# Loads at the start of a transformer block: three through GpSimd's DMA queue, and larger single DMAs for x and the key weights

## The chip, the cores and the metric

The kernel runs on one core of a Trainium2 chip. The metric is device time in microseconds, from the start of the program to its end. A core has five engines that run side by side, each with its own instructions in a fixed order: TensorE (matrix products; PE in the profile, its weight loads PEld), VectorE (DVE), ScalarE (ACT), GpSimd (POOL) and SyncE (SP), which here only starts DMA transfers. Engines wait for each other through semaphores. A transfer is started by one of the engines (its queue) and then moved by 16 DMA engines that all queues share.

## The reference

One transformer block with adaptive layer norm. x has 2048 tokens of 512 values, all in bf16.

```python
mod = (silu(c) @ w_mod).reshape(1, 6, 1, -1)          # c: 1 x 512, w_mod: 512 x 3072
sa, ca, ga, sb, cb, gb = mod[:, 0], ..., mod[:, 5]
h = layernorm(x) * (1 + ca) + sa
x = x + ga * attention(h, wqkv, w_phi, wo)
h = layernorm(x) * (1 + cb) + sb
x = x + gb * ((silu(h @ w_gate) * (h @ w_up)) @ w_down)
```

The attention is linear: 32 heads of 16 values. Queries and keys go through w_phi (16 x 16 for each head), then through two softmaxes over these 16 values, one of them with the sign turned; keys times values are summed over all tokens, and each query reads that sum.

## The kernel before

**Tiles and stages.** The tokens are cut into four chunks of 512 (`x_ch[0]` to `x_ch[3]`), each of four tiles of 128. In the first stage w_phi is folded into the key and the query weights (`fold_phi`: transposes at line 540, products at line 551), x is normalized (`first_norm`), transposed by TensorE (`first_T`, line 447) and scaled and shifted by `modA`, which holds 1 + ca and sa as columns. Then each tile gives its keys (line 613), values (line 617) and its share of the sum of keys times values (line 649), and each chunk its queries (line 673). The second stage is attention, output projection, second norm and the feed-forward network, which takes most of the time (lines 906 and 978).

**What stands first on TensorE.** Products of c with a one turn the row c into columns (line 471, `f_cT`); then w_phi is spread over the partitions (line 519, `f_phx`), the key weights are transposed in four groups (line 540), and the first fold is made (line 551). Then follow the four steps that make `modA` out of w_mod's first part, one for each block of 128 rows of w_mod (line 492, `mod_cols`), mixed with two more folds; then the first transposes of normalized x (line 447). Without modA no `hT`, the transposed and scaled x, can be written, and without `hT` no projection can start.

**The planner.** Each engine's order is not found on the chip: `Plan.run` walks a list, `ORDER`, and gives every operation a planned start, from the planned ends of what it needs, from the durations written at each operation (`us=`), and from the due times (`at`) of what is loaded. A due time comes from `load`: it adds up the bytes of the loads in the order in which they stand in the program, at 315 GB/s until 8 us and at 375 GB/s after that, from 3.1 us on, whichever queue the load goes to. c and w_phi have fixed due times, 4.5 and 4.1. The order of an engine's work does not depend on due times, since `ORDER` sets it.

**The filler.** Before each step of TensorE, `fill` puts matmuls of a tile of ones (line 1046) whose result is not used; they keep TensorE busy while it would wait. How many there are is fixed when the program is built, from the gap between the planned end of the step before and the planned start of this one:

```python
left = int((o.start - t0 + 0.05) * (1200 if t0 < 7.0 else 2400))
while left >= 64:
    fns.append(lambda n=min(left, CW): f(n))
    left -= CW
```

`left` counts columns, `CW` is 512, `t0` is the planned end of the step before. This form is used until the first product of keys and values (line 649).

**Loads.** ScalarE's queue starts w_phi and c. SyncE's queue starts, in this order: the first chunk of x in two halves, the key weights in two halves, w_mod's first part (columns 0 to 1023, the shift and the scale of the first norm) in four blocks of rows, the value weights, the second chunk of x in two halves, the query weights, the third and the fourth chunk of x. The wait of a step is on all that it reads: the transposes of key weights at line 540 need the half that holds their rows, the statistics of x at line 384 need the half of the chunk that holds their tile, and the steps at line 492 need silu(c) and their block of w_mod. The transposes of the query weights are DMA transposes on SyncE's queue (line 321), behind these loads.

Of the kernel before, what the change touches and what calls it, by code (L numbers as in the profile page):

```python
# [20 lines left out]
D = 512  # L21
KD = D // P
# [183 lines left out]
def kernel(  # L206
# [14 lines left out]
    nc = tc.nc  # L221
    ctx.enter_context(tc.manual_schedule())

    x_v = A_x.flatten_outer_dims().rearrange("(c p t) d -> c p t d", p=P, t=TPC)
    out_v = out.flatten_outer_dims().rearrange("(c p t) d -> c p t d", p=P, t=TPC)
    wqkv_v = A_wqkv.rearrange("(k p) n -> p k n", p=P)
    wmod_v = w_mod.rearrange("(k p) n -> p k n", p=P)
# [46 lines left out]
    x_ch = [attn.tile([P, TPC, D], BF16, name=f"x_c{i}") for i in range(NCH)]  # L274
    wqkv_sb = wts.tile([P, KD, 3 * D], BF16, name="wqkv_sb")
# [6 lines left out]
    wphi_sb = wts.tile([P, KD * DH], BF16, name="wphi_sb")  # L282
    c_row = const.tile([1, D], BF16, name="c_row")
# [3 lines left out]
    wmod_sb = modp.tile([P, KD, 6 * D], BF16, name="wmod_sb")  # L287
# [5 lines left out]
    def load(eng, dst, src, kb):  # L293
        eng.dma_start(dst, src)
        landed[0] += kb * 1024 / (315e3 if landed[0] < 8 else 375e3)
        return landed[0]

    nc.scalar.dma_start(wphi_sb[:], A_w_phi.rearrange("h (q t) f -> (h q) (t f)", t=4))
    nc.scalar.dma_start(c_row[:], c[:, :])
    at_x = {}  # L300
    at_x[0, 0] = load(nc.sync, x_ch[0][:, 0:2, :], x_v[0][:, 0:2, :], 256)
    at_x[0, 1] = load(nc.sync, x_ch[0][:, 2:4, :], x_v[0][:, 2:4, :], 256)
    at_wk = [load(nc.sync, wqkv_sb[:, i:i + 2, D:2 * D], wqkv_v[:, i:i + 2, D:2 * D], 256) for i in range(0, KD, 2)]
    at_m1 = [load(nc.sync, wmod_sb[:, k, 0:2 * D], wmod_v[:, k, 0:2 * D], 256) for k in range(KD)]
    landed[0] += 0.9
    at_wv = load(nc.sync, wqkv_sb[:, :, 2 * D:3 * D], wqkv_v[:, :, 2 * D:3 * D], 512)
    at_x[1, 0] = load(nc.sync, x_ch[1][:, 0:2, :], x_v[1][:, 0:2, :], 256)
    at_x[1, 1] = load(nc.sync, x_ch[1][:, 2:4, :], x_v[1][:, 2:4, :], 256)
    at_wq = load(nc.sync, wqkv_sb[:, :, 0:D], wqkv_v[:, :, 0:D], 512)
    at_x[2] = load(nc.sync, x_ch[2][:], x_v[2], 512)  # L310
    at_x[3] = load(nc.sync, x_ch[3][:], x_v[3], 512)
# [29 lines left out]
    nc.gpsimd.memset(mhalf[:], -0.5)  # L341
    eps_t = const.tile([P, 1], FP32, name="eps")
    nc.gpsimd.memset(eps_t[:], LN_EPS)

    nc.scalar.add_instruction(mybir.InstLoadActFuncSet(name=nc.get_next_instruction_name(), act_func_set_id=6,
                                                       ins=[], outs=[]))
# [365 lines left out]
    for i in range(NT):  # L712
        c_i, t = divmod(i, TPC)
# [372 lines left out]
```

The softmax here doesn't subtract the row's maximum and nothing guards it: scores larger than these inputs give would overflow.

## Time and profile before

| | before |
|---|---|
| time, median of 2 runs | 208.63 us (208.31 to 208.96) |
| span of the profiled execution | 207.3 us |
| TensorE busy (fillers included) | 202.4 us, 98% |
| VectorE, ScalarE, GpSimd busy | 143.1, 114.0, 131.0 us |
| filler at line 1046 in the first 30 us | 13.3 us |
| key weights, first half, started and landed | 1.64 us, 6.19 us |
| first step of w_mod on TensorE (line 492) | 8.7 us |
| first projection (line 617) | 13.2 us |

A busy TensorE is not a useful TensorE here: the fillers count as busy. The chain of waits, which follows the work that ended last back to the start, says what each stretch of time hangs on. The timeline lists instructions in order of time, runs of equal ones merged: start, duration, engine, line, operation, tile written and tiles read, sizes, and how many.

### The profile page before, as it was taken

The numbers are of one execution on the slowest core, as the hardware profiler recorded it, in microseconds if no ns is written. First come the engines' busy times: TensorE is split into PE (matmuls) and PEld (weight loads), VectorE is DVE, ScalarE is ACT, GpSimd is POOL, SyncE is SP. The second block draws the span as 40 slices with busy tenths as digits, with TensorE's granted clock in tenths as the row PEclk, the third lists the DMA queues.
The fourth block names the chain that finished last, engine by engine and source line by source line (L and its number), as shares of the span: only waits on it lengthen the run. The fifth ranks groups of instructions, "written<-read, shape, count | busy, mean of one in ns | idle before, by whom it ended". The sixth has DMA issues, their size and how long they took to land.

```text
span 207.3 us, 4949 instructions
## 1 busy us (share of the span) xinstructions
PE 202.4 (98%) x1876; PEld 140.0 (68%) x1876; DVE 143.1 (69%) x351; ACT 114.0 (55%) x244; POOL 131.0 (63%) x172
## 2 busy tenths in 40 slices
PE   7999999999999999999999999999999999999994
PEld 2764656454555698785887876879675787698752
DVE  6699899999676886999789687887467222322232
ACT  2689999998789974335452542422532564044300
POOL 1069999899991546689678793677749254061451
PEclk9999999999999999999999999999999999999999
DMA  5996993797000011231611233202321330020012
GB/s 176 335 389 119 321 191 87 275 406 254 4 0 0 3 25 36 51 81 26 91 32 28 58 83 81 57 0 60 79 62 28 79 85 3 13 66 27 0 34 68
DMA packets 34025, 19.76 MB, mean 95 GB/s; under 512 B 25073, under 2 KB 30674, under 8 KB 34002
## 3 DMA queue, kind: packets, MB, share of 16 engines
q1 hardware_dynamic: 33712, 19.38, 33.5%
q8 instruction: 14, 0.23, 0.5%
q10 hardware_dynamic: 290, 0.08, 0.2%
q14 instruction: 9, 0.07, 0.1%
HBM read 11.58 MB, written 2.10 MB: 66 GB/s over the span
## 4 chain that ended last, share of the span: by engine, by line
PE 92%; DMA 2%; ACT 1%; POOL 1%; DVE 1%; SPq 0%; issue 0%; DVEq 0%
PE one_ps L906 34%; PE one_ps L978 18%; PE one_ps L852 7%; PE one_ps L613 6%; PE one_ps L673 6%; PE one_ps L617 5%; PE four_ps L781 4%; PE one_ps L948 3%; PE kv_ps L1046 2%; DMA wqkv_sb<-in_A_wqkv_dram 2%; PE kv_ps L649 2%; PE one_ps L447 1%; PE one_ps L551 1%; PE one_ps L540 1%; ACT e L624 1%; POOL phik L642 1%
## 5 line engine op out<-in xcount | busy, mean ns | idle before, releaser
L978 PE MATMUL one_ps<-wd_sb,gu 128*128 128x512 bf16 (+2 forms) x176 | 41.0, 372 | 0.0
L906 PE MATMUL one_ps<-hT,wg_sb 128*128 128x256 bf16 (+1 forms) x400 | 41.0, 251 | 0.0
L906 PE MATMUL one_ps<-hT,wu_sb 128*128 128x256 bf16 (+1 forms) x400 | 40.9, 251 | 0.0
L913 ACT ACTIVATE sg<-one_ps 128x512 bf16<-128x512 f32 (+1 forms) x42 | 23.7, 576 | 27.6 <-PE one_ps L906 26.4
L906 PEld LDWEIGHTS <-wg_sb 128*128 128x128 bf16 x400 | 32.7, 98 | 4.8
L906 PEld LDWEIGHTS <-wu_sb 128*128 128x128 bf16 x400 | 32.9, 98 | 4.2
L916 DVE TENSOR_TENSOR gu<-one_ps,sg 128x512 bf16<-128x512 f32 (+1 forms) x26 | 16.6, 640 | 22.1 <-PE one_ps L906 12.8
L642 POOL TENSOR_TENSOR phik<-e,R 128x1024 bf16<-128x1024 bf16 x16 | 30.5, 1930 | 1.1 <-ACT eT L679 0.7
L922 POOL TENSOR_TENSOR gu<-usb,sg 128x512 bf16<-128x512 bf16 x16 | 18.5, 1155 | 16.8 <-ACT sg L913 13.3
L978 PEld LDWEIGHTS <-gu 128*128 128x128 bf16 (+1 forms) x187 | 17.7, 98 | 15.0
L384 DVE BATCH_NORM_STATS2 st<-x_c 128x6 f32<-128x512 bf16 x32 | 21.3, 682 | 1.4 <-DMA x_c<-in_A_x_dram 1.1
L994 POOL TENSOR_TENSOR ot<-x_c,fg 128x512 bf16<-128x512 bf16 (+1 forms) x14 | 15.7, 1118 | 8.8 <-DVE fg L990 8.8
L839 POOL TENSOR_TENSOR o<-o 128x512 bf16<-128x512 bf16 x14 | 16.1, 1154 | 7.6 <-DVE o L819 7.1
L819 DVE TENSOR_TENSOR o<-four_ps,A 128x512 bf16<-128x512 f32 x32 | 20.5, 683 | 0.0
L634 DVE TENSOR_REDUCE S<-e 128x64 f32<-128x1024 bf16 x16 | 19.0, 1194 | 0.6 <-ACT e L624 0.4
L624 ACT ACTIVATE e<-one_ps 128x512 bf16<-128x512 f32 x32 | 17.7, 631 | 1.6 <-POOL phik L642 1.0
L990 DVE TENSOR_TENSOR fg<-one_ps,gab 128x512 bf16<-128x512 f32 (+1 forms) x16 | 10.7, 672 | 11.5 <-PE one_ps L978 10.8
L679 ACT ACTIVATE eT<-one_ps 128x512 bf16<-128x512 f32 x32 | 17.5, 628 | 1.4 <-PE one_ps L673 1.3
L920 ACT CAST usb<-one_ps 128x512 bf16<-128x512 f32 x16 | 9.3, 586 | 16.3 <-PE one_ps L906 14.4
L852 PE MATMUL one_ps<-wo_sb,oT 128*128 128x512 bf16 x64 | 16.1, 379 | 0.0
L617 PE MATMUL one_ps<-wqkv_sb,hT 128*128 128x512 bf16 x64 | 15.9, 379 | 0.1
L673 PE MATMUL one_ps<-hT,Wq 128*128 128x512 bf16 x64 | 15.6, 379 | 0.1
(117 smaller groups left out, 311.2 us busy)
## 6 DMA issues: line engine op xcount, KB each, us to landing
wmod_sb<-in_w_mod_dram SPq DMA_DIRECT2D x2, 1024.0 KB, 7.0
out_dram<-ot SPq DMA_DIRECT2D x15, 128.0 KB, 2.0
wg_sb<-in_B_w_gate_dram SPq DMA_DIRECT2D x1, 1376.0 KB, 8.3
wu_sb<-in_B_w_up_dram SPq DMA_DIRECT2D x1, 1376.0 KB, 11.3
wd_sb<-in_B_w_down_dram SPq DMA_DIRECT2D x1, 1280.0 KB, 14.4
x_c<-in_A_x_dram SPq DMA_DIRECT2D x4, 256.0 KB, 4.7
wmod_sb<-in_w_mod_dram SPq DMA_DIRECT2D x4, 256.0 KB, 5.7
wqkv_sb<-in_A_wqkv_dram SPq DMA_DIRECT2D x2, 512.0 KB, 7.1
```

The lines of the kernel that those rows point to most:

```text
L384: pl.op("DVE", r=reads, w=[st6], us=0.6, fn=lambda: nc.vector.bn_stats(st6()[:], src))
L617: nc.tensor.matmul(v()[:], lhsT=hT[c_i][k][:, cols], rhs=wqkv_sb[:, k, 2 * D:3 * D], start=(k == 0), stop=(k == KD - 1))
L624: nc.scalar.activation(e()[:, :, sg].rearrange("p g h f -> p g (h f)"), pk()[:].rearrange("p (g n) -> p g n", g=G), ACT.Exp, scale=(1.0, - ...
L634: pl.op("DVE", r=[e], w=[Ss], us=1.14, fn=lambda: nc.vector.tensor_reduce(Ss()[:], e()[:].rearrange("p g s h f -> p (g s h) f"), axis=AX.X ...
L642: pl.op("POOL", r=[e, R], w=[bphik[i]], us=1.92, fn=lambda: nc.gpsimd.tensor_tensor(bphik[i]()[:].rearrange("p g s h f -> p (g s h) f"), e ...
L673: nc.tensor.matmul(pq()[:], lhsT=Wq2[:, k, j * P:(j + 1) * P], rhs=hT[c_i][k][:], start=(k == 0), stop=(k == KD - 1))
L819: nc.vector.tensor_tensor(o2()[:, sg].rearrange("p j (h d) -> p j h d", d=DH), ndv()[:, :, sg, 0:P].rearrange("p j (h d) -> p j h d", d=DH ...
L852: nc.tensor.matmul(a()[:], lhsT=oT()[:, j, :], rhs=wo_sb[:, j, :], start=(j == 0), stop=(j == KD - 1))
L906: nc.tensor.matmul(ps_()[0:fsz, q * n:(q + 1) * n], lhsT=wt[:, k, m * P:m * P + fsz], rhs=h2[k], start=(k == 0), stop=(k == KD - 1))
L913: pl.op("ACT", r=[g, btab], w=[sg], us=0.08 + 0.41 * L / CW, fn=lambda: nc.scalar.activation(sg()[0:fsz, 0:L], g()[0:fsz, 0:L], ACT.Silu))
L922: pl.op("POOL", r=[usb, sg], w=[gu], us=0.17 + 0.98 * L / CW, fn=lambda: nc.gpsimd.tensor_tensor(gu()[0:fsz, 0:L], usb()[0:fsz, 0:L], sg() ...
L978: nc.tensor.matmul(fp()[:], lhsT=b()[0:fsz, c0:c0 + P], rhs=wd_[0:fsz, m, wcs], start=(m == 0), stop=(m == FM - 1))
```

## The change

Four loads leave their queues. c and w_phi go from ScalarE's queue to GpSimd's, behind GpSimd's few constants. w_mod's first part goes from SyncE's queue to GpSimd's, in two halves instead of four blocks; its lines also move to a later place in the program, behind all first loads of SyncE. The first chunk of x, the second chunk of x and the key weights are loaded in one DMA each instead of two. The purpose is to have fewer and larger transfers at the start, and to let a third queue start some of them, so that SyncE and ScalarE get to their next work sooner.

```diff
-    nc.scalar.dma_start(wphi_sb[:], A_w_phi.rearrange("h (q t) f -> (h q) (t f)", t=4))
-    nc.scalar.dma_start(c_row[:], c[:, :])
     at_x = {}
-    at_x[0, 0] = load(nc.sync, x_ch[0][:, 0:2, :], x_v[0][:, 0:2, :], 256)
-    at_x[0, 1] = load(nc.sync, x_ch[0][:, 2:4, :], x_v[0][:, 2:4, :], 256)
-    at_wk = [load(nc.sync, wqkv_sb[:, i:i + 2, D:2 * D], wqkv_v[:, i:i + 2, D:2 * D], 256) for i in range(0, KD, 2)]
-    at_m1 = [load(nc.sync, wmod_sb[:, k, 0:2 * D], wmod_v[:, k, 0:2 * D], 256) for k in range(KD)]
+    at_x[0, 0] = at_x[0, 1] = load(nc.sync, x_ch[0][:], x_v[0], 512)
+    at_wk = [load(nc.sync, wqkv_sb[:, :, D:2 * D], wqkv_v[:, :, D:2 * D], 512)] * 2
     landed[0] += 0.9
     at_wv = load(nc.sync, wqkv_sb[:, :, 2 * D:3 * D], wqkv_v[:, :, 2 * D:3 * D], 512)
-    at_x[1, 0] = load(nc.sync, x_ch[1][:, 0:2, :], x_v[1][:, 0:2, :], 256)
-    at_x[1, 1] = load(nc.sync, x_ch[1][:, 2:4, :], x_v[1][:, 2:4, :], 256)
+    at_x[1, 0] = at_x[1, 1] = load(nc.sync, x_ch[1][:], x_v[1], 512)
     at_wq = load(nc.sync, wqkv_sb[:, :, 0:D], wqkv_v[:, :, 0:D], 512)
     at_x[2] = load(nc.sync, x_ch[2][:], x_v[2], 512)
     at_x[3] = load(nc.sync, x_ch[3][:], x_v[3], 512)
...
     eps_t = const.tile([P, 1], FP32, name="eps")
     nc.gpsimd.memset(eps_t[:], LN_EPS)
+    nc.gpsimd.dma_start(c_row[:], c[:, :])
+    nc.gpsimd.dma_start(wphi_sb[:], A_w_phi.rearrange("h (q t) f -> (h q) (t f)", t=4))
+    at_m1 = [load(nc.gpsimd, wmod_sb[:, i:i + 2, 0:2 * D], wmod_v[:, i:i + 2, 0:2 * D], 512) for i in (0, 0, 2, 2)[::2]]
+    at_m1 = [at_m1[0]] * 2 + [at_m1[1]] * 2
```

## The prediction

> **What bounds the kernel now.** I read the page first (shares, chain), then the chain in order of time, then the timeline of the first 27 us, then busy time by stretches of 5 us.
>
> ```profile
> PE 92%; DMA 2%; ACT 1%; POOL 1%; DVE 1%; SPq 0%; issue 0%; DVEq 0%
> ```
>
> Nearly all of the span is a chain on TensorE, which works through its instructions in one fixed order. So whatever is put into that order early moves everything behind it. The chain in order of time shows the part that the change touches:
>
> ```profile
> 1.64 4.55 DMA wqkv_sb<-in_A_wqkv_dram
> 6.24 1.04 PE one_ps L540 x8
> ...
> 8.93 0.19 PE one_ps L492 x8
> 9.12 0.53 PE kv_ps L1046 x2
> 9.65 0.19 PE one_ps L492 x8
> ...
> 10.80 0.18 PE one_ps L492 x8
> ...
> 13.36 0.86 PE one_ps L617 x4
> ...
> 22.40 0.76 PE kv_ps L1046 x4
> ```
>
> The first key weights land at 6.19 us. L540 transposes them, L492 multiplies silu(c) with w_mod's first part (four steps, 8.93 to 10.98), and L617 at 13.36 is the first real projection. In between stands L1046: the filler, matmuls of ones that keep TensorE busy. It is no idle time that later work may use: TensorE must execute it. Its length is written into the program by the planner, from the due times (`at`) of the loads. The timeline shows the lengths:
>
> ```profile
> 7.07 0.29 PE L1046 MATMUL kv_ps<-ones 128*128 128x98 bf16 x1
> 8.98 0.67 PE L1046 MATMUL kv_ps<-ones 128*128 128x512 bf16 x2
> 10.51 0.29 PE L1046 MATMUL kv_ps<-ones 128*128 128x307 bf16 x1
> ```
>
> I check the formula of `fill` on these: columns = (planned start of the next step - planned end of the last + 0.05) x 1200, or x 2400 once the planned time is past 7.0 us. Key weights' second half is due at 6.43 and the transposes before it end at 6.40 in the plan: 0.08 x 1200 = 98 columns, as the first row has. w_mod's row block 3 is due at 9.49 and the step before ends at 9.41: 307 columns, the third row. So the plan's gaps can be read off the trace, and new due times give new gaps by the same formula.
>
> Beyond 25 us no slack stands in the early stage:
>
> ```profile
> 20.00:25.00 5.00, 5.00 (x53) 3.39 (x52) 4.30 (x14) 4.68 (x12) 5.00 (x5) 1.00 0.85 273
> 25.00:30.00 5.00, 5.00 (x38) 2.67 (x36) 5.00 (x15) 4.94 (x13) 4.83 (x3) 1.00 1.20 243
> 30.00:35.00 5.00, 5.00 (x66) 2.98 (x65) 4.90 (x7) 5.00 (x10) 4.89 (x5) 1.00 0.42 91
> ```
>
> The columns after the length are busy us of PE, PEld, DVE, ACT and POOL. All are near 5.00 of 5.00, so a late start can't be caught up there.
>
> **What the Trainium skill says.** "DMA: Bandwidth & Descriptors", Issuing engines are not separate DMA queues: transfers started from several engines run on the same 16 DMA engines and interleave, so another queue saves only issue time. The trace of before shows that issue time (four issues of w_mod take 2.10 us of SyncE) and moves 326 GB/s from 5 to 10 us, so bytes are the limit there. The same page, Latency and other measured facts: first byte after about 1 us from GpSimd's queue and 0.6 us from the other two; and Anatomy of one DMA, SWDGE: about 2.0 us of fixed cost per transfer. Before has no data load on GpSimd, so neither is shown; from ScalarE's queue w_phi took 3.2 us to land. "TensorE: Matmul & The Clock Gate", Part 1: 1.2 GHz cold and 2.4 GHz after about 3.4 us of sustained work, 215.7 ns for one warm matmul of 512 columns. The trace agrees: weight loads shorten from 150 to 98 ns near 8.8 us, and four matmuls of 512 take 0.86 us.
>
> **The change part by part.**
>
> Fewer and larger transfers on SyncE (x in one, key weights in one, w_mod gone). SyncE's issues for x and key weights drop from four (0.87 + 0.94 us) to two, so the key weights are issued near 1.2 us. Both halves must land now before the first transpose. Before, 174 GB/s x 5 us = 870 KB had moved by 5.0 us, 786 KB stand up to the first half, and it landed at 6.19; the second half was taken up at 7.27. The whole, 1049 KB with the first chunk of x, with less mixed in, I estimate at 6.2 to 7.3, say 6.9. The value weights, the second chunk of x and the query weights come earlier than before; nothing waits for them at that point, so no gain, with one exception: at 22.40 the filler of 0.76 us stands in the plan before the second query fold, because the transposes of the query weights on SyncE are planned from 16.08 us (query weights due 14.58 + 1.5). They become due at 11.79 + 1.5, and TensorE reaches this place later, so that filler shrinks. GpSimd, busy 5.00 of 5.00 there, and ScalarE, 4.68, limit what that gives: between 0 and 0.8, I take -0.4 us.
>
> c and w_phi through GpSimd. GpSimd's last constant is set at 1.38 us, so c is issued near 1.4 and w_phi behind it. At 1 us + 2 us each, with w_phi's issue about 1 us after c's, c lands at about 4.5 to 5.5 and w_phi at 5 to 7. I take 5.7 for the later of the two (4.8 and 5.0 is where their steps on TensorE stand now). Behind them wait, on TensorE in order, c's columns (L471), w_phi's spread (L519, 0.62 us both together), then filler, then the transposes of the key weights. This filler grows too: the transposes are due at 6.43 instead of 5.60, their predecessor ends in the plan at 5.2, so (1.23 + 0.05) x 1200 = 1536 columns, three matmuls at 0.43 cold = 1.3 us. Transposes start at 5.7 + 0.5 + 1.3 = 7.5 against 6.24: +1.3 us. (If w_phi lands at 5.0: 6.9, set by the key weights, +0.7. At 7.0: 8.8, +2.6.)
>
> w_mod's first part: the load moves behind all of SyncE's loads in program order, so `landed` counts it last. I follow `landed`: 3.10; x 4.76; key weights 6.43; +0.9; value weights 8.99; x's second chunk 10.39; query weights 11.79; third and fourth chunk 13.19 and 14.59; w_mod's halves 15.98 and 17.38. Before, its four blocks were due at 7.26, 8.09, 8.79 and 9.49. These are only due times; the bytes will be there long before (3.5 MB at 326 GB/s from 2 us gives about 13 us for everything up to the query weights and w_mod together). But the due times set the filler. The step before the first w_mod step is the first phi fold (L551), planned at 8.03 now (four transposes of 0.40 from 6.43), ending 8.37. Filler: (15.98 - 8.37 + 0.05) x 2400 = 18,400 columns, 35 matmuls of 512 and one of some 470: 35 x 0.2157 + 0.2 = 7.75 us of TensorE where before 120 columns (0.1 us) stood. That is +7.65 us, on the path: behind it in TensorE's order wait all four w_mod steps, then modA, the first hT, and from there every projection. VectorE's and ScalarE's next work (L497, L455, L458) needs modA, and what is behind in their queues waits with it, so no other engine gets ahead meanwhile.
>
> From the first w_mod step to L617 the fillers were 600+120+120+120+307+218 columns and become about 120x3+312+120x2: 570 columns less, -0.23 us.
>
> Sum: +1.3 + 7.65 - 0.23 - 0.4 = +8.3 us; 208.63 + 8.3 = 216.9 us. Warmth: if TensorE's pause before c keeps it cold some us longer, half of that comes on top (0 to 1 us); not in the sum, but in the range.
>
> **The rivals.**
>
> (1) Forecast, planned filler holds TensorE: 214.5 to 219, chance 0.70. For it: the columns of the trace follow the formula exactly.
>
> (2) GpSimd's queue is the worse bound: c and w_phi land at 8 to 10 us and the cold clock lasts. "SBUF — State Buffer" in the skill, the box on the "DVE blocks DMA" trap, says that GpSimd can't write descriptors while VectorE runs an operation that takes the port they share; VectorE's casts and memsets of 1.3 to 2.6 us stand beside these four loads, and no load here shows what they cost it. Then +2 to +5 more: about 220, chance 0.16. For it: L471 stands first in TensorE's order and everything queues behind it. Against: these operations last 0.2 to 0.5 us each and end at 2.6.
>
> (3) Later slack swallows most: fillers of 20 to 24 us (2.73 us in that stretch) vanish wholly, +7 to +5 stays: about 212.5, chance 0.08. Against: those gaps follow normalizations of the second chunk that stand behind modA on VectorE and move with it.
>
> (4) Not slower: the due times don't lengthen the filler, or the stretch is filled with other work. Then the start gains at most what the 4.55 us wait for key weights loses, some 1 us: 207.7, chance 0.06. For it: value weights and x's second chunk really come earlier. Against: nothing in the order stands between the fold and w_mod's steps that could fill it.
>
> **How the numbers follow.** The likeliest is (1), 216.9. Range 213.5 to 220.5: its lower end takes c early (+0.7) and the filler at 22 us wholly saved with some of the next, its upper w_phi at 7 us and 1 us of cold clock; that leaves out (4), most of (3) and the upper part of (2), about 2 in 10. The 2% bound above is 212.8: slower takes (1), (2) and half of (3), 0.90; same takes the other half and part of (4), 0.07; faster 0.03.
>
> **What would show it.** Right: on the timeline a block of some 36 matmuls of 512 columns at L1046 between L551 and the first L492, 7.7 us long, w_mod's DMA landed before its end; first L492 near 18 us instead of 8.7, first L617 near 22 instead of 13.2; the stretch after that like before, shifted. L471 waiting for c after 4.9 us. Wrong: L492 waits for the DMA itself after the filler (then GpSimd's queue is the cause), the filler block is short, or the first kv tiles start late but the span at 60 us has caught up.

## The result and the profile after

| | before | after |
|---|---|---|
| time, median of 2 runs | 208.63 us | 220.55 us (220.02 to 221.08) |
| ratio to before | | 1.0572 (95% interval 1.05 to 1.0644) |
| span of the profiled execution | 207.3 us | 219.2 us |
| w_phi used on TensorE | 5.0 us | 8.5 us |
| key weights' transposes start (chain) | 6.24 us | 10.37 us |
| first w_mod step (chain) | 8.93 us | 21.51 us |
| first projection (chain) | 13.36 us | 25.42 us |

The kernel became slower by 11.9 us. The direction was as forecast, and the block of filler too; the size was not: 216.9 us was predicted, with 220.5 as the upper end, and c and w_phi landed later than the sum had them. In the changed kernel line numbers are lower by one: the filler is L1045, the w_mod steps L491, the first projection L616. The shares of its chain, from the page:

```profile
PE 93%; DMA 3%; issue 1%; DVE 1%; POOL 1%; ACT 0%; POOLq 0%; DVEq 0%
```

DMA has 3% where it had 2%, and the chain in order of time says which transfer it is now. The columns are start, duration, and what the time hangs on:

```profile
2.23 6.20 DMA wphi_sb<-in_A_w_phi_dram
...
8.48 0.60 PE one_ps L518 x16
9.07 1.29 PE kv_ps L1045 x3
10.37 0.85 PE one_ps L539 x8
...
12.38 0.43 PE one_ps L550 x4
12.80 0.22 issue
13.02 8.49 PE kv_ps L1045 x35
21.51 0.18 PE one_ps L491 x8
...
25.42 0.86 PE one_ps L616 x4
...
34.28 0.81 PE kv_ps L1045 x4
```

Two things are new. The key weights no longer lead the chain: a load of 16 KB does, w_phi, which takes 6.20 us to land. And between the first fold (L550) and the first w_mod step stands one block of filler of 8.49 us (35 matmuls are on record; the plan has 36). From there to the end little differs: the first projection stands 12.06 us later than before, the end 11.9 us.

The list of DMA issues gives size and us from issue to landing; here w_phi before and after:

```profile
wphi_sb<-in_A_w_phi_dram ACTq DMA_DIRECT2D x1, 16.0 KB, 3.2
```

```profile
wphi_sb<-in_A_w_phi_dram POOLq DMA_DIRECT2D x1, 16.0 KB, 6.2
```

c took 5.6 us. The timeline of the changed kernel shows TensorE's two pauses, for c and for w_phi, in brackets:

```profile
7.13 0.25 PE L470 MATMUL one_ps<-ones,c_row 1*128 1x1 bf16 x4 [2.45 <-DMA c_row<-in_c_dram]
8.48 0.60 PE L518 MATMUL one_ps<-wphi_sb,spread 128*128 128x16 bf16 x16 [1.10 <-DMA wphi_sb<-in_A_w_phi_dram]
```

The same in busy time by stretches of 5 us (busy us of PE, PEld, DVE, ACT and POOL with the number of instructions; then the granted TensorE clock, the DMA share and GB/s), one stretch of before and then three of after:

```profile
5.00:10.00 5.00, 4.82 (x67) 3.89 (x65) 3.59 (x14) 3.22 (x9) 0.00 (x0) 1.00 0.98 326
```

```profile
5.00:10.00 5.00, 1.77 (x23) 1.11 (x24) 2.02 (x7) 0.17 (x1) 0.00 (x0) 0.78 1.03 370
10.00:15.00 5.00, 4.78 (x30) 3.39 (x30) 2.07 (x8) 3.05 (x8) 0.00 (x0) 0.54 1.03 387
15.00:20.00 5.00, 5.00 (x25) 2.23 (x23) 0.00 (x0) 0.00 (x0) 0.00 (x0) 1.00 0.68 87
```

From 5 to 10 us TensorE works 1.77 of 5 us (4.82 before). From 10 to 15 us its granted clock is 0.54 in this profile. From 15 to 20 us it is the only engine that works, and what it does is filler: VectorE, ScalarE and GpSimd have not one instruction. The next work of VectorE and of ScalarE is to copy the second fold's result (L554, L553), and that fold stands on TensorE behind the block: they wait 9.2 and 8.6 us for it.

### The profile page after: what moved, and what is told of

Read it like the earlier page. It is cut to its first block, busy times and chain, and to the rows that moved or that the text cites. A ratio compares the mean times of both kernels' runs of the same rounds, so it can differ in the third digit from the quotient of the medians.

```text
span 219.2 us, 4991 instructions
## 1 busy us (share of the span) xinstructions
PE 209.2 (95%) x1885; PEld 143.8 (66%) x1911; DVE 142.9 (65%) x351; ACT 113.9 (52%) x244; POOL 133.7 (61%) x176
## 4 chain that ended last, share of the span: by engine, by line
PE 93%; DMA 3%; issue 1%; DVE 1%; POOL 1%; ACT 0%; POOLq 0%; DVEq 0%
PE one_ps L905 32%; PE one_ps L977 16%; PE one_ps L616 6%; PE kv_ps L1045 6%; PE one_ps L672 6%; PE one_ps L612 6%; PE one_ps L851 6%; PE four_ps L780 4%; DMA wphi_sb<-in_A_w_phi_dram 3%; PE one_ps L947 3%; PE kv_ps L648 2%; PE one_ps L446 1%; PE one_ps L550 1%; PE one_ps L539 1%; PE one_ps L691 1%
## 5 line engine op out<-in xcount | busy, mean ns | idle before, releaser
L977 PE MATMUL one_ps<-wd_sb,gu 128*128 128x512 bf16 (+2 forms) x165 | 39.3, 372 | 0.5
L1045 PE MATMUL kv_ps<-ones 128*128 128x512 bf16 (+8 forms) x82 | 21.5, 370 | 1.7 <-DVE ones L320 1.4
L433 POOL TENSOR_SCALAR xn<-x_c,ln_mv,ln_nmr 128x512 bf16<-128x512 bf16 x10 | 7.6, 772 | 19.3 <-DVE ln_nmr L419 19.1
L612 PE MATMUL one_ps<-Wk,hT 128*128 128x512 bf16 x61 | 15.5, 379 | 0.4 <-issue 0.2
```

Source lines behind the costliest of these rows:

```text
L612: nc.tensor.matmul(pk()[:], lhsT=hT[c_i][k][:, cols], rhs=Wk2[:, k, :], start=(k == 0), stop=(k == KD - 1))
L977: nc.tensor.matmul(fp()[:], lhsT=b()[0:fsz, c0:c0 + P], rhs=wd_[0:fsz, m, wcs], start=(m == 0), stop=(m == FM - 1))
L1045: nc.tensor.matmul(dst, lhsT=ones[:, 0:P], rhs=src, start=early or late, stop=True, skip_group_check=True)
```

## The experiments

Ratios are to the kernel before on the same chip, with their 95% intervals.

### Where the 12 us come from

**Due times set back, transfers as in the changed kernel**

```diff
-    at_m1 = [at_m1[0]] * 2 + [at_m1[1]] * 2
+    at_m1 = [7.26, 8.09, 8.79, 9.49]
```

> The changed kernel, with w_mod's due times set back to 7.26, 8.09, 8.79 and 9.49; the transfers stay as they are. Theory A (the block of filler is made by the due times alone; w_mod's bytes are there by 12.3 us): no block, the first w_mod step follows the first fold at about 13 us, first L616 near 17.3 instead of 25.4, time about 212.5: 8 us of the 12 go, 4 stay (the late c and w_phi). Theory B (w_mod through GpSimd's queue is itself late and TensorE would wait for it anyway): the block turns into a wait for the DMA, time stays at 217 to 220.

Measured 211.94 us, ratio 1.0157 (1.0121 to 1.0194). The chain of this kernel where the block stood:

```profile
11.39 0.43 PE one_ps L550 x4
11.82 0.10 PE kv_ps L1045
11.92 0.19 PE one_ps L491 x8
```

No block and no wait: at 11.9 us w_mod is there. So 8.6 of the 11.9 us (220.55 - 211.94) are filler that four numbers in the planner wrote, and not a transfer. Theory A holds, B falls.

**Due times alone, on the kernel before**

```diff
     at_m1 = [load(nc.sync, wmod_sb[:, k, 0:2 * D], wmod_v[:, k, 0:2 * D], 256) for k in range(KD)]
+    at_m1 = [15.98, 15.98, 17.38, 17.38]
```

> The kernel before, with nothing changed but the due times of w_mod's four blocks: 15.98, 15.98, 17.38, 17.38. No transfer moves. Theory A (the planner's filler is executed in full and nothing behind it catches up): a block of 36 matmuls before the first L492, first L617 7.2 to 7.7 us later, time about 216. Theory B (later slack takes in much of it): below 213.

Measured 215.89 us, ratio 1.0342 (1.0305 to 1.0379). In its chain the block is

```profile
7.77 0.22 PE one_ps L552 x4
8.00 8.56 PE kv_ps L1047 x40
16.56 0.18 PE one_ps L493 x8
```

40 matmuls and not the 36 of my expectation, since in this kernel the fold ends at 7.57 in the plan: (15.98 - 7.57 + 0.05) x 2400 = 20,300 columns. The first projection (20.46 us) is 7.1 us later than before and the time 7.4 us longer than the 208.49 measured beside it: what is put in before modA reaches the end in full.

**c and w_phi back on ScalarE's queue**

```diff
+    nc.scalar.dma_start(wphi_sb[:], A_w_phi.rearrange("h (q t) f -> (h q) (t f)", t=4))
+    nc.scalar.dma_start(c_row[:], c[:, :])
     at_x = {}
...
-    nc.gpsimd.dma_start(c_row[:], c[:, :])
-    nc.gpsimd.dma_start(wphi_sb[:], A_w_phi.rearrange("h (q t) f -> (h q) (t f)", t=4))
```

> The changed kernel, with c and w_phi back on ScalarE's queue as its first instructions. Theory A (late c and w_phi cost what they delay the transposes, 10.37 against 6.24 us, less the longer filler before them): c and w_phi are used at 4.8 to 5.0 us, transposes start near 7.0, the block of filler stays, 7.7 us long since TensorE is warm sooner; time about 217. Theory B (c and w_phi are late only beside a wait that is there anyway, for the joined key weights): transposes still start after 9 us, time 219.5 to 220.5.

Measured 214.87 us, ratio 1.0297 (1.0259 to 1.0336), less than either theory had. Its chain:

```profile
5.62 1.14 PE kv_ps L1045 x3
6.76 0.45 PE one_ps L539 x8
...
7.81 0.25 PE one_ps L550 x4
8.06 7.75 PE kv_ps L1045 x36
15.81 0.18 PE one_ps L491 x8
```

The transposes start at 6.76, and they take 1.05 us to the fold where they took 2.01 in the changed kernel; the block takes 7.75 us, as worked out in the prediction, instead of 8.49 with one matmul fewer on record. So moving two small loads back is worth 5.7 us: 3.6 us because TensorE starts its transposes earlier, most of the rest because its matmuls then run at full pace (eight transposes in 0.45 us, and 0.85 us in the changed kernel).

**Both set back: joined loads and w_mod on GpSimd's queue stay**

The edit is that of the two kernels above together.

> Both: due times of before, c and w_phi on ScalarE's queue; what stays of the change is w_mod on GpSimd's queue in two halves and the joined loads of x and key weights. Theory A (due times and the two small loads are the whole loss): 208.5 to 209.5, the same as before within 1%. Theory B (the joined loads or w_mod's queue cost something of their own): 211 or more.

Measured 209.99 us, ratio 1.0074 (1.005 to 1.0098): between the theories. Its timeline shows what is left:

```profile
8.57 0.35 PE L491 MATMUL one_ps<-silucT,wmod_sb 128*128 128x1 bf16 x8 [1.10 <-DMA wmod_sb<-in_w_mod_dram]
10.91 0.35 PE L491 MATMUL one_ps<-silucT,wmod_sb 128*128 128x1 bf16 x8 [1.05 <-DMA wmod_sb<-in_w_mod_dram]
```

With block and late c gone, TensorE waits 1.10 and 1.05 us for w_mod's two halves. So the move of w_mod does cost something too; in the changed kernel the filler hides it. Whether it is the queue, or that the steps now wait for halves and not for four blocks, no run separates. The size is rough: in 6 of the 20 runs the mean granted clock was 0.991 or 0.992 and the time 211.17 to 211.81 us, in the other 14 it was at least 0.998 and the time 208.97 to 210.21. The profile is one of the six; the median of the 14, 209.66, is 0.6% above 208.49.

**Joined loads alone**

```diff
-    at_x[0, 0] = load(nc.sync, x_ch[0][:, 0:2, :], x_v[0][:, 0:2, :], 256)
-    at_x[0, 1] = load(nc.sync, x_ch[0][:, 2:4, :], x_v[0][:, 2:4, :], 256)
-    at_wk = [load(nc.sync, wqkv_sb[:, i:i + 2, D:2 * D], wqkv_v[:, i:i + 2, D:2 * D], 256) for i in range(0, KD, 2)]
+    at_x[0, 0] = at_x[0, 1] = load(nc.sync, x_ch[0][:], x_v[0], 512)
+    at_wk = [load(nc.sync, wqkv_sb[:, :, D:2 * D], wqkv_v[:, :, D:2 * D], 512)] * 2
...
-    at_x[1, 0] = load(nc.sync, x_ch[1][:, 0:2, :], x_v[1][:, 0:2, :], 256)
-    at_x[1, 1] = load(nc.sync, x_ch[1][:, 2:4, :], x_v[1][:, 2:4, :], 256)
+    at_x[1, 0] = at_x[1, 1] = load(nc.sync, x_ch[1][:], x_v[1], 512)
```

> The kernel before, with only the joined loads of x (first and second chunk) and of the key weights; c, w_phi and w_mod stay on their queues, due times follow from the loads' order as before. Theory A (the joined loads cost nothing: the longer filler of three matmuls before the transposes ends near 6.8 us, when the key weights are there, and TensorE is warm sooner): 208 to 209, within 0.5% of before. Theory B (waiting for the whole of the key weights costs 0.6 us or more, as the second half was taken up at 7.27 us): 209.2 to 210.

Measured 208.02 us beside 208.26, ratio 0.9991 (0.9979 to 1.0003). No difference can be told. Alone, the joined loads cost nothing; the loss is in the moved loads, in the due times that moved with them, and in what the joined loads add to late small ones (below).

### Why c and w_phi land late

**At the head of GpSimd's queue**

```diff
     ident_f = const.tile([P, P], FP32, name="ident_f")
+    nc.gpsimd.dma_start(c_row[:], c[:, :])
+    nc.gpsimd.dma_start(wphi_sb[:], A_w_phi.rearrange("h (q t) f -> (h q) (t f)", t=4))
     nc.gpsimd.memset(ident_f[:], 0.0)
...
-    nc.gpsimd.dma_start(c_row[:], c[:, :])
-    nc.gpsimd.dma_start(wphi_sb[:], A_w_phi.rearrange("h (q t) f -> (h q) (t f)", t=4))
```

> The changed kernel, with c and w_phi still on GpSimd's queue but ahead of all its constants, at 0.7 and 1.45 us, before SyncE's bulk has begun to move. Theory Q: they land like on ScalarE's queue, 3.2 to 4 us after their issue, at 4.5 to 5.5 us; time near 215 to 216. Theory S: 5.6 to 6.2 us after their issue as in the changed kernel, w_phi at 7.0 to 7.7; time near 219.

Measured 219.36 us, ratio 1.0523 (1.0446 to 1.0599). The issue was not where I wanted it: c at 1.25 us instead of 0.7, only 0.24 us ahead of the changed kernel and after the start of SyncE's first two issues (0.72 and 1.18). c and w_phi landed 4.8 and 5.2 us after their issue, between the theories. By itself it decides nothing, but it is the right kernel to hold the next one against.

**Nothing of SyncE beside them**

```diff
     at_x = {}
+    scratch = const.tile([P, KD * DH], BF16, name="scratch")
+    nc.gpsimd.dma_start(c_row[:], c[:, :])
+    nc.gpsimd.dma_start(wphi_sb[:], A_w_phi.rearrange("h (q t) f -> (h q) (t f)", t=4))
+    nc.sync.dma_start(scratch[:], wphi_sb[:])
...
-    nc.gpsimd.dma_start(c_row[:], c[:, :])
-    nc.gpsimd.dma_start(wphi_sb[:], A_w_phi.rearrange("h (q t) f -> (h q) (t f)", t=4))
```

> The changed kernel, with c and w_phi at the head of GpSimd's queue and all of SyncE's first loads held back until w_phi has landed (SyncE first copies w_phi to an unused tile), so that no bulk of SyncE runs beside them; the program starts later on purpose and only the landing of c and w_phi counts. Theory Q: c and w_phi land 2 to 3.5 us after their issue. Theory S: 5 us or more, also with the DMA engines idle.

From the lists of DMA issues, the kernel above, and then this one:

```profile
c_row<-in_c_dram POOLq DMA_DIRECT2D x1, 1.0 KB, 4.8
wphi_sb<-in_A_w_phi_dram POOLq DMA_DIRECT2D x1, 16.0 KB, 5.2
```

```profile
c_row<-in_c_dram POOLq DMA_DIRECT2D x1, 1.0 KB, 1.9
wphi_sb<-in_A_w_phi_dram POOLq DMA_DIRECT2D x1, 16.0 KB, 1.9
```

Same engine, same queue, same bytes, c issued at 1.25 and at 1.26 us, VectorE's first casts from 3.20 us on in both: 1.9 us without SyncE's loads, 4.8 and 5.2 with them. So GpSimd's queue isn't slow in itself (theory S falls); the loads are held up by SyncE's bulk. The trace of the changed kernel agrees. From 4 to 5 us, some 2 us and more after c's issue was over (2.23), SyncE's queue is the only one that moves anything,

```profile
DMA packets 363, 0.36 MB, mean 358 GB/s; under 512 B 13, under 2 KB 363, under 8 KB 363
q1 hardware_dynamic: 363, 0.36, 104.9%
```

and the first packets of GpSimd's queue run in the microsecond after. (The time of this kernel, 222.4 us in one run, means nothing, as it starts its bulk late on purpose.)

**On ScalarE's queue, further down in its program**

```diff
     nc.scalar.add_instruction(mybir.InstLoadActFuncSet(...))
+    nc.scalar.dma_start(c_row[:], c[:, :])
+    nc.scalar.dma_start(wphi_sb[:], A_w_phi.rearrange("h (q t) f -> (h q) (t f)", t=4))
...
-    nc.gpsimd.dma_start(c_row[:], c[:, :])
-    nc.gpsimd.dma_start(wphi_sb[:], A_w_phi.rearrange("h (q t) f -> (h q) (t f)", t=4))
```

> The changed kernel, with c and w_phi on ScalarE's queue, but behind its table load, so that they are issued at about 2.0 and 2.5 us, when SyncE's bulk loads are already running (on GpSimd's queue: 1.5 and 2.2 us). Theory Q (they are late because they run on the same 16 DMA engines behind bulk): w_phi lands 5.5 us or more after its issue, at 8 us or later, time near 219 to 220. Theory S (GpSimd's queue starts slowly by itself; its first packets ran at 5.0 us): w_phi lands 3.2 to 4.0 us after its issue, at 5.7 to 6.5, time near 216.

Measured 216.26 us, ratio 1.0374 (1.0284 to 1.0464). This was to be a test of ScalarE's queue at 2.0 us, but the table load does not hold up the issue: c went out at 0.75 and w_phi at 1.30 us. w_phi landed 4.3 us after its issue. The kernel to hold this against is the one with c and w_phi back on ScalarE's queue, which has the same bulk: there it was issued at 0.72 us and took 3.9. So 0.6 us of later issue cost 0.4 us. The packets of ScalarE's queue (q10) ran from 4 to 5 us, beside SyncE's, and none ran from 2 to 4 us:

```profile
q1 hardware_dynamic: 329, 0.33, 95.6%
q10 hardware_dynamic: 125, 0.01, 9.8%
```

It decides nothing: the timing is not the planned one, the difference is small, and theory S expected 3.2 to 4.0 us.

**Only c and w_phi moved**

```diff
-    nc.scalar.dma_start(wphi_sb[:], A_w_phi.rearrange("h (q t) f -> (h q) (t f)", t=4))
-    nc.scalar.dma_start(c_row[:], c[:, :])
...
     nc.gpsimd.memset(eps_t[:], LN_EPS)
+    nc.gpsimd.dma_start(c_row[:], c[:, :])
+    nc.gpsimd.dma_start(wphi_sb[:], A_w_phi.rearrange("h (q t) f -> (h q) (t f)", t=4))
```

> The kernel before, with only c and w_phi moved to GpSimd's queue (behind its constants, as in the changed kernel); every other load and every due time as before. Theory Q (they start behind the bulk of SyncE and land late for that reason, whatever the shape of that bulk): c is used near 6.5 to 7.5 us, w_phi near 7 to 8.5, transposes 2 to 3 us later than before, time 211 to 212. Theory J (the lateness comes from the joined loads with their longer rows): c and w_phi land by 5.5 us and time is 208.5 to 209.5.

Measured 209.87 us, ratio 1.0078 (1.0053 to 1.0102): slower, but by 1.6 us only. Both loads land 3.9 us after their issue, c is used at 5.4 and w_phi at 6.2. Neither theory had this: both loads land earlier than Q said, and the time is above what J said. In the changed kernel, behind the joined loads, they take 5.6 and 6.2 us.

**The joined loads, and c and w_phi moved**

The edit is that of the joined loads and of the kernel above together.

> The joined loads and c and w_phi on GpSimd's queue; w_mod stays on SyncE's queue in four blocks, due times as before. Which of the two raises the landing of c and w_phi from 3.9 us after issue (only they moved) to 5.6 and 6.2 (the changed kernel)? Theory J (the joined loads): 5 us or more after issue, w_phi used at 7.7 or later, time about 210.5 to 211.5. Theory G (w_mod's two loads right behind them on GpSimd's own queue): 3.9 us, w_phi used near 6.2, time 209 to 209.9.

Measured 212.67 us, ratio 1.0187 (1.0164 to 1.0209). The list of DMA issues, of the kernel above and of this one:

```profile
c_row<-in_c_dram POOLq DMA_DIRECT2D x1, 1.0 KB, 3.9
wphi_sb<-in_A_w_phi_dram POOLq DMA_DIRECT2D x1, 16.0 KB, 3.9
```

```profile
c_row<-in_c_dram POOLq DMA_DIRECT2D x1, 1.0 KB, 4.9
wphi_sb<-in_A_w_phi_dram POOLq DMA_DIRECT2D x1, 16.0 KB, 5.0
```

Joined loads cost nothing alone (0.9991), but with c and w_phi behind them they turn 0.8% into 1.9%. Landing is only a part of that. Against the kernel above w_phi is used 1.08 us later (7.25 us), and the filler ahead of the transposes is 0.85 us longer (1.29 for 0.44 us, three matmuls for one): the key weights, due as a whole at 6.43, write it, and late c and w_phi put it on the path. Both theories had too short a time.

How far are landings of one profile each to be trusted? Three kernels have the same transfers in the same order, the changed one, the one with due times set back and the one with added filler (further below). In them c took 5.6, 6.1 and 5.2 us, w_phi 6.2, 5.6 and 5.8. So single landings scatter by up to 0.9 us, and the step from 4.9 and 5.0 here to 5.6 and 6.2 in the changed kernel, with w_mod on GpSimd's queue as the other difference, is not clear of that.

**One of the two joined loads taken apart, the rest as in the changed kernel.** First x's first chunk, then the key weights:

```diff
-    at_x[0, 0] = at_x[0, 1] = load(nc.sync, x_ch[0][:], x_v[0], 512)
+    at_x[0, 0] = load(nc.sync, x_ch[0][:, 0:2, :], x_v[0][:, 0:2, :], 256)
+    at_x[0, 1] = load(nc.sync, x_ch[0][:, 2:4, :], x_v[0][:, 2:4, :], 256)
```

```diff
-    at_wk = [load(nc.sync, wqkv_sb[:, :, D:2 * D], wqkv_v[:, :, D:2 * D], 512)] * 2
+    at_wk = [load(nc.sync, wqkv_sb[:, i:i + 2, D:2 * D], wqkv_v[:, i:i + 2, D:2 * D], 256) for i in range(0, KD, 2)]
```

> The changed kernel, with the first chunk of x in two halves again (rows of 2 KB instead of 4 KB in one piece). Theory L (the long rows of x ahead of them hold c and w_phi back): c and w_phi land about 4 us after their issue, time near 217. Theory D (what counts is how many bytes SyncE has started by then, whatever their rows): 5 us or more, time 219 to 220.5.

> The changed kernel, with the key weights in two halves again (rows of 1 KB in both forms). Theory L: no difference, c and w_phi land 5.5 us or more after issue, time 220 to 221. Theory D: SyncE starts the value weights half a microsecond later, so landing is a few tenths of a microsecond sooner, 5.2 to 5.6, time 219.5 to 220.5.

Measured 219.12 us (ratio 1.0493, 1.0456 to 1.053) and 219.95 us (1.0532, 1.0499 to 1.0566). c landed 4.6 and 4.2 us after its issue (5.6 in the changed kernel), w_phi 5.7 and 5.5 (6.2). Theory L expected about 4 for both loads and a time near 217 with x in halves; the time and w_phi are against it. The times lie where theory D, that the amount started ahead counts, had them (219 to 220.5, 219.5 to 220.5), but c landed sooner than D said in both, and most of the differences lie within the scatter of 0.9 us. So neither theory is shown, and how the engines share their turns is not settled.

### Does the pause slow TensorE's clock?

```diff
             left = int((o.start - t0 + 0.05) * (1200 if t0 < 7.0 else 2400))
+            left += 5 * CW if o.n == 0 else 0
```

> The changed kernel with five more matmuls of 512 columns of filler ahead of c's step, which bridge the pause from 4.9 us to c's landing at 7.1 us; nothing else moves. Theory W (the pause drops TensorE's clock, and the slow clock costs 1.0 us between transposes and first fold and 0.7 us in the block of filler): block 7.75 us, first fold 1 us after the transposes, time 218.6 to 219.2. Theory N (the clock has nothing to do with the pause): 220.5, the added filler being hidden in the wait.

Measured 218.03 us, ratio 1.0481 (1.0449 to 1.0514), though TensorE executes five matmuls more than in the changed kernel. Its four runs (217.82 to 219.57) lie below both runs of that kernel, but the intervals of the two ratios just overlap. Granted clock from 5 to 10 and from 10 to 15 us:

```profile
5.00:10.00 5.00, 3.49 (x36) 2.01 (x34) 2.42 (x10) 0.17 (x1) 0.00 (x0) 0.88 1.03 371
10.00:15.00 5.00, 5.00 (x33) 3.21 (x32) 1.61 (x5) 3.05 (x8) 0.00 (x0) 0.78 1.04 393
```

0.88 and 0.78 instead of 0.78 and 0.54. The block is 7.94 us long (8.49, and 0.22 of idle time before it) and the filler ahead of the transposes 0.97 (1.29): 1.1 us less in these two profiles. The transposes to the fold still take 2.01 us, so only a part of what theory W named came; 0.45 us more is an earlier landing of w_phi in this profile (8.03), which the added filler can't cause.

Is it the granted clock? Other runs show slow matmuls without a lowered one. The kernel in which only c and w_phi moved has pauses of 0.56 and 0.47 us for them and a granted clock of 1.00 throughout, and its eight transposes take the 0.85 us of the changed kernel and not 0.45:

```profile
5.00:10.00 5.00, 4.09 (x53) 3.62 (x54) 3.21 (x13) 2.44 (x9) 0.00 (x0) 1.00 1.04 374
7.21 0.85 PE one_ps L540 x8
```

With c and w_phi at the head of GpSimd's queue the granted clock is 1.00 from the start to 20 us too, with pauses of 1.21 and 0.94 us, and still the transposes to the fold take 2.01 us and the block 8.64. And the changed kernel's second run had a mean granted clock of 0.999, where the profiled one had 0.984, and its span was 218.1 us instead of 219.2: the lower clock goes with 1.1 us at most.

What the traces show is a pace. Each of these kernels starts with matmuls of 0.43 us for 512 columns, half of the later pace of 0.216. They reach full pace by 6.8 us with c and w_phi on ScalarE's queue and no pause, by 9.9 us before (one pause of 0.18 us), by 11.1 us where only c and w_phi moved, and within the block, after 13 us, in the changed kernel. That fits slow matmuls after pauses, as theory W has it, with another sign than the granted clock. Which pause is long enough, and that the pause is the cause, is not shown: with c and w_phi on ScalarE's queue further down, a pause of 0.89 us was followed by full pace at 6.9 us.

### A version that might beat both

```diff
-            left = int((o.start - t0 + 0.05) * (1200 if t0 < 7.0 else 2400))
+            left = int((o.start - t0) * (1200 if t0 < 7.0 else 2400))
```

This is on top of the joined loads alone.

> The kernel with only the joined loads, and without the 0.05 us that the filler's formula adds to each gap, so that no 120 columns stand where the plan has no gap. Theory A (filler is executed in full and on the path, some 18 times 0.05 us in the first 24 us): 0.6 to 0.9 us less, 207.2 to 207.6 where before has 208.3. Theory B (the filler stands where TensorE would wait for another engine anyway): no difference, 208.

Measured 207.83 us beside 208.25, ratio 0.9989 (0.997 to 1.0007): the interval holds 1, so no gain is shown. The gain exists at the start: the first step of attention on TensorE begins at 56.80 us in the chain instead of 58.20 with the joined loads alone. In the profiled run, whose 208.66 us are 0.8 above the median, it is given back later, in one wait on TensorE between 70 us and the end that the other kernel doesn't have:

```profile
PE one_ps L850 <- DVE o L817: 1.4, 1, 1.4
```

Whether the other runs have this wait is not known; the median lies between the two theories.

## Why the prediction was wrong in size and right in kind

The working gave +8.3 us; the two chains differ by 11.9 us:

| step | predicted | measured from the chains |
|---|---|---|
| transposes of the key weights start later | +1.3 | 10.37 - 6.24 = +4.13 |
| transposes to first fold | 0 | 2.01 - 2.16 = -0.15 |
| first fold to first w_mod step (the block) | +7.65 | (21.51 - 12.38) - (8.93 - 8.40) = +8.60 |
| first w_mod step to first projection | -0.23 | 3.91 - 4.43 = -0.52 |
| first projection to the end | -0.4 | 193.78 - 193.94 = -0.16 |
| sum | +8.3 | +11.9 |

**The block: right.** Due times at 15.98 and 17.38 wrote it, and it shows where and as the prediction said, 0.95 us longer than predicted; the due times alone give 1.0342 on the kernel before. w_mod's bytes were there before: with the due times set back its first step ran at 11.92 us without a wait.

**The step that failed is "I take 5.7 for the later of the two".** w_phi was used at 8.48 us, 2.8 us later, and that is most of the 3.6 us by which the sum was short. From w_phi on the step was right: 0.6 us of products and 1.29 us of filler bring the transposes to 10.37. The estimate added the two prices of the Trainium skill's page "DMA: Bandwidth & Descriptors", about 1 us of first byte (Latency and other measured facts) and 2 us of fixed cost (Anatomy of one DMA). In the quiet kernel a whole landing took 1.9 us, near the fixed cost alone. Beside bulk it took longer: 3.9 us beside the old loads, 4.9 and 5.0 beside the joined ones, 4.2 to 6.2 with w_mod on the same queue as well. I had quoted the same page (Issuing engines are not separate DMA queues) on transfers that share 16 engines and interleave, and used it only against a gain for w_mod, not as a cost for a load of 1 KB that goes out at 1.49 us, when SyncE has started one load of 512 KB at 0.73 and is issuing the next. Nor did the loads interleave at first: from 2.23 us, the end of c's issue, to 5 us no packet of GpSimd's queue ran, and SyncE's moved about 1 MB. Rival (2) came near the size ("c and w_phi land at 8 to 10 us", "about 220") with another reason in hand, VectorE beside the writing of descriptors. With c and w_phi issued before VectorE's casts they still took 4.8 and 5.2 us, so VectorE is not the main cause; the 0.8 to 1.0 us to the changed kernel's landings are about the size of the scatter.

**Warmth was left out of the sum.** The prediction put 0 to 1 us in the range. The block is 0.95 us longer than predicted: 8.49 us, and 0.22 of idle time before it, for 7.75 at full pace. Against the kernel with c and w_phi on ScalarE's queue, the changed kernel loses 0.96 us between transposes and fold and 0.74 us in the block to slow matmuls. So a late first load seems to cost twice, its own wait and slow matmuls after it; that the pause makes them slow is likely and not shown.

**Later slack: smaller than taken.** The filler at 22.40 us in the kernel before is still there, at 34.28 us, 0.81 us instead of 0.76. My -0.4 came from earlier due query weights; the gap stayed, so in the plan it hangs on something else, which I did not trace.

**The losses together.** Due times alone cost 3.4%, the late loads with joined ones 1.9%: 5.3% of the 5.7% (5.0 to 6.4) measured, so these two account for it within the noise. The move of w_mod cost 0.6 to 0.8% (joined loads 0.9991, with w_mod on GpSimd's queue 1.0074); it is hidden in the changed kernel, because the block is longer than the wait.

**Three readings of the working that don't hold.** TensorE worked from 1.44 us on with one gap of 0.18 us and was at half pace past 9 us, so the trace of before does not agree with 3.4 us to full speed. 326 GB/s was not a limit of bytes: from 10 to 15 us the kernel before moved 403 GB/s. And the range's upper end does not follow from its terms: w_phi at 7 us (+2.6), the block, 1 us of cold clock and no gain later give 208.63 + 2.6 + 7.65 - 0.23 + 1 = 219.7, not 220.5.

What stays open: how the DMA engines share their turns, and so why the two forms of bulk differ. The runs show how much, not by which rule.

## What to carry to other kernels

A due time in a planner is not a comment: where it writes filler or fixes an order, moving a load in the program is an edit of the schedule, and it is executed even if the data come early. A small load that many wait for belongs ahead of the bulk; a free queue does not make it early. Before a load's fixed price is used, ask what is already started on the same engines at that moment.

## What the runs showed of the hardware

A load of 1 KB started on GpSimd's queue landed after 1.9 us with no other traffic, and after 3.9 to 6.1 us beside SyncE's loads in the eight other kernels that had it there; three kernels with the same transfers gave 5.2, 5.6 and 6.1. On ScalarE's queue a load of 16 KB issued at 0.72 us, together with SyncE's first load, took 3.1 and 3.2 us beside loads in halves and 3.5 to 3.9 us beside the joined ones, and 4.3 us beside these when issued at 1.30. ScalarE's table load of 1.28 us (0.72 to 2.00) did not hold back the two transfers that stand behind it in its program: they were issued at 0.75 and 1.30. TensorE's matmuls ran at half pace, 0.43 us for 512 columns, from their start, and after pauses of 0.56 and 0.47 us still at 10 us, though the granted clock in the records was 1.00.
